# Turning the inverse row sums of a group, and placing its normalised sums, each one slot later in a hand-ordered pipeline

## Chip, cores and metric

The kernel runs on one NeuronCore of a Trainium2 chip. The metric is the device time in microseconds, as the median of several executions; one more execution is recorded by the hardware profiler. All rows below come from that one.

## What is computed

For 8 batches and 8 heads of 576 rows with head width 64, the scores of every row against the 576 keys are formed, all but the 32 largest of a row are dropped, the rest is put through a softmax and multiplied with v. The heads are laid side by side as x (576 rows by 512 per batch), and a channel mix follows, whose input blends each row with the row before it:

```
scores = scale * q @ k.T
kth    = the 32nd largest of each row
attn   = softmax(where(scores >= kth, scores, -1e9))     # row sums + 1e-9 below
x      = (attn @ v), heads side by side
xk, xr = mu*x + (1-mu)*x_prev, for mu_k and mu_r
out    = sigmoid(xr @ w_r) * (relu(xk @ w_k)**2 @ w_v)
```

## The kernel before, in words

**Groups, tiles and slots.** The 4608 rows of all batches are cut in 18 pieces of 256 rows; a piece and a pair of heads make a group, 72 in all. A group has four tiles of 128 partitions (64 rows of each of two heads or row blocks, by 576 scores). There are 288 tiles, and the loop of `pipeline` (line 713) takes one new tile per pass; a pass is called a slot here. Slot n works on tiles of several ages: it forms the scores of tile n, the candidates of tile n-1, the best of tile n-2, the sign count of tile n-3, the exponentials and the threshold mask of tile n-4, and it turns tile n-5 on TensorE (line 284). Each slot emits its steps in the order of the list ORDER (line 43), written out by hand; every engine runs what it was given strictly in that order.

**The row sums.** The mask (L274, VectorE) leaves the masked exponentials and their row sums. Let t be the slot of the last tile of a group. In slot t+5 the four columns of row sums get 1e-9 added (L291, ScalarE), are inverted (L294, VectorE), and each inverse is spread over 64 columns (L298, GpSimd) into the tile rb. In slot t+6 four transposes on TensorE turn rb (L305, `turn_inverse`) into the upper columns of the PSUM tile pt, in which the same slot has just turned another tile; ScalarE moves the result to the tile ri (L309) after it has moved the turned tile (L287). In the same slot, at its end, 40 matmuls weigh v with the turned exponentials of the group (L318). In slot t+7 ScalarE moves those sums out of PSUM (L322), and GpSimd multiplies them by ri (L326, `place`) into xT, the transposed x.

**The channel mix.** It runs beside this, in chunks of 256 rows. A chunk has 8 pieces of gate matmuls (pz), 16 of hidden (ph) and 16 of value (pv), 40 in all; `work` (line 661) lets some into each slot, by a budget of TensorE time per slot (3.45) of which scores, turns, the weighing (1.38) and the turned inverses (0.16) take their part first. Their element-wise steps are queued with a cost on ScalarE ("act") and GpSimd ("pool"), and let in by similar budgets. A half of a chunk may begin once the groups of its two pairs of heads are placed: `state["heads"]` is set in the step place (line 863), and the step mix of the same slot, which comes later in ORDER, looks at it. In the last 36 slots the charge per piece falls from 0.72 to 0.56 (line 673), so that up to four go into a slot. From slot total + 4 on, VectorE takes over from GpSimd for the mix.

**Buffers.** pt has one buffer, so the next slot's turn waits until ScalarE has moved out what lies in it. rb has one buffer, ri and the sums two.

The steps that matter stand in ORDER in this sequence (others left out): count, below, exp, norm, evac, score, turn, inv, keep, sums, bounds, eighth, norm2, et, late, act, thr, mask, place, mix, weigh, dve, pool, judge. "below" is GpSimd's product of scores and signs (L263), "eighth" VectorE's next eight of it (L828), and "late" the move to ri.

Of the kernel before, what the change touches and what calls it, by code (L numbers as in the profile page):

```python
# [46 lines left out]
def topk_attention_channel_mix(ctx: ExitStack, tc: tile.TileContext, q, k, v, mu_k, mu_r, w_k, w_v, w_r, out):  # L47
# [148 lines left out]
    def open_group(P):  # L196
# [4 lines left out]
        for t in range(4):  # L201
            T = Env()
            T.P, T.t, T.u, T.j = P, t, t // 2, t % 2
            T.last = t == 3
            P.tiles.append(T)

    hs = [slice(e * 64, (e + 1) * 64) for e in range(2)]

    def scores(g, P, T):
        x, (Q, R) = T.u * 128, P.blocks[T.u]  # L210
        if Q is R:
            for e, h in enumerate(hs):
                nc.tensor.matmul(g.ps[:, e], lhsT=P.qs[h, T.j, x:x + 128], rhs=Q.K[h, T.j], start=True, stop=True)  # L213
        else:
            for i, N in enumerate((Q, R)):
                for e, h in enumerate(hs):
                    nc.tensor.matmul(g.ps[hs[i], e], lhsT=P.qs[h, T.j, x + i * 64:x + (i + 1) * 64], rhs=N.K[h, T.j], start=True, stop=True)
        return g.ps
# [81 lines left out]
    def turn_inverse(g, P, L):  # L300
        rb = P.rb.rearrange("p (u h) d -> p u (h d)", u=2)
        pr = g.pt[:, :, 384:]
        for u in range(2):
            for n, h in enumerate(hs):
                nc.tensor.transpose(pr[:, n, u * 64:(u + 1) * 64], rb[h, u], ident[h, h])  # L305

        def out_():
            P.ri = g.two.tile([128, 256], F32, name="ri")
            nc.scalar.activation(P.ri.rearrange("p (u n q) -> p n u q", u=2, n=2), pr.rearrange("p n (u q) -> p n u q", u=2), AF.Copy)  # L309
        L.at(0, "late", out_)  # L310
# [13 lines left out]
    def place(P, Q):  # L324
        rows, cols = slice(1 + Q.row, 1 + Q.row + Q.m), slice(Q.c0, Q.c0 + Q.m)
        nc.gpsimd.tensor_mul(Q.xT[:, P.hp, rows], P.sum[:, cols], P.ri[:, cols])  # L326
# [266 lines left out]
    def new_batch(g, b=0):  # L593
        x = g.one.tile([128, HP, 1 + S], F32, name="xT", tag=f"x{b % 2}")
        nc.gpsimd.memset(x[:, :, 0:1], 0.0)
        return x

    def pipeline(g):
        L = Lanes()
# [25 lines left out]
        xT, tiles, state = {}, {}, {"heads": [0] * HP, "wait": 0, "start": 0, "held": [], "K": {}}  # L625

        def save(size=CH):

            b, s = divmod(state["start"], S)
            if s > S - size and not state["held"]:  # L630
                m = S - s
                rest = g.one.tile([128, HP, CH - 63], F32, name="rest")
                nc.gpsimd.tensor_scalar(rest[:, :, :m + 1], xT[b][:, :, s:], 1.0, 1.0, op0=OP.mult, op1=OP.mult)
                state["held"] = [(rest, 0, m)]
# [69 lines left out]
        total = 4 * len(groups)  # L704
# [5 lines left out]
        state["K"][Q.b, P.hp] = Q.K  # L710
        load_mu(L)
        n = 0
        while n < total + 8 or "next" in state or L.busy():
            if n == total + 4:
                g.by, L.rate = nc.vector, 0.5
            A, C, B_, M, V, W = (tiles.get(n - d) for d in (1, 2, 3, 4, 5, 6))
            X = tiles.get(n - EXPS)
            last = W if W and W.last else None
# [38 lines left out]
            def inv():  # L757
                if last:
                    L.use("pe", 1.38)
                if last:  # L760
                    if not V:
                        g.pt = g.psT.tile([128, 2, 512], F32, name="pt")
                    turn_inverse(g, W.P, L)
                    L.use("pe", 0.16)
                    L.use("act", 0.25)

# [77 lines left out]
                    L.use("pool", 0.6)  # L844

            def place_():
                T = tiles.get(n - 7)
                if T and T.last:
                    P = T.P
                    for Q in P.parts:  # L850
                        if Q.b not in xT:
                            if state["start"] < (Q.b - 1) * S:
                                save()
                            C = state["chunk"]
                            assert C.pieces is None or C.begun == 4 or C.first > Q.b - 2
                            assert state["start"] + sum(h[2] for h in state["held"]) >= (Q.b - 1) * S
                            if Q.b > 1:
                                for read in g.reads.values():
                                    L.force(read)
                            xT[Q.b] = new_batch(g, Q.b)  # L860
                        Q.xT = xT[Q.b]
                        place(P, Q)
                    state["heads"][P.hp] = (P.p + 1) * ROWS
                if V and V.last and V.P.last:
                    nc.vector.tensor_reduce(least[:, V.P.p:V.P.p + 1], V.P.group[:, :, :, 23::9], axis=mybir.AxisListType.XYZ, op=OP.min)

            def judge():
                if n == total + 6:
# [4 lines left out]
                    nc.vector.tensor_scalar(flag, lowest, TINY, None, op0=OP.is_lt)  # L873

            do = dict(loads=loads, judge=judge, score=score, turn=turn_, inv=inv, exp=exp, weigh=weigh_, norm=norm, norm2=norm2, bounds=bounds_,
                      count=count_, below=below_, keep=keep_, mix=mix, eighth=eighth, thr=thr, mask=mask_, place=place_, sums=sums, weights=weights)
            do.update({f"c{c}": lambda c=c: cands(c, c + 1) for c in range(NCH)})
            do.update({f"best{r}": lambda r=r: ranks_(best, r) for r in range(3)})
# [10 lines left out]
    with ExitStack() as stack:  # L889
        g = Env()  # L890
        open_pools(stack, g, "")
        stack.enter_context(tc.manual_schedule())
        pipeline(g)
# [3 lines left out]
    with tc.If(again > 0):  # L897
        with tc.For_i(0, B, 1) as b, ExitStack() as stack:
            g = Env()
            g.staged, g.by = (lambda: True), nc.gpsimd  # L900
            open_pools(stack, g, "_again")
            L = Direct()
# [70 lines left out]
```

## Time and profile before

| | us |
|---|---|
| median of 3 runs | 1178.5 (1176.14 to 1180.02) |
| the profiled execution, device time | 1177.31 |
| its span, first to last instruction | 1175.5 |
| TensorE busy with matmuls | 1089.7 (93%) |
| TensorE busy with weight loads | 850.1 (72%) |
| VectorE busy | 1072.5 (91%) |
| ScalarE busy | 966.8 (82%) |
| GpSimd busy | 959.8 (82%) |
| mean granted TensorE clock | 0.982 of full |

The device time holds 1.8 us that lie outside the span. Busy time is a mean over a start (weights are split there, and TensorE has less to do), a long steady part, and an end in which the mix has no attention beside it. The steady part repeats every 16 slots, which is four groups and one chunk.

### The profile page before, as it was taken

The numbers are of one execution on the slowest core, as the hardware profiler recorded it, in microseconds if no ns is written. First come the engines' busy times: TensorE is split into PE (matmuls) and PEld (weight loads), VectorE is DVE, ScalarE is ACT, GpSimd is POOL, SyncE is SP. The second block draws the span as 40 slices with busy tenths as digits, with TensorE's granted clock in tenths as the row PEclk, the third lists the DMA queues.
The fourth block names the chain that finished last, engine by engine and source line by source line (L and its number), as shares of the span: only waits on it lengthen the run. The fifth ranks groups of instructions, "written<-read, shape, count | busy, mean of one in ns | idle before, by whom it ended". The sixth has DMA issues, their size and how long they took to land.

```text
span 1175.5 us, 32787 instructions
## 1 busy us (share of the span) xinstructions
PE 1089.7 (93%) x10753; PEld 850.1 (72%) x10753; DVE 1072.5 (91%) x5959; ACT 966.8 (82%) x1969; POOL 959.8 (82%) x1011
## 2 busy tenths in 40 slices
PE   5678898999999999999999999999999999999897
PEld 2344676868787878787878777878787878777776
DVE  6999999999999999999999999999999998899732
ACT  5898998979897989898989888989898988787721
POOL 4798897888988898989898989898989798787810
PEclk9888999999999999999999999999999999999899
DMA  6433223323332333222221233323232323211000
GB/s 177 133 113 111 54 74 90 81 55 83 84 81 61 79 77 85 59 54 55 71 57 52 57 81 83 78 70 84 76 88 65 86 70 79 78 40 49 11 20 21
DMA packets 168275, 85.86 MB, mean 73 GB/s; under 512 B 126112, under 2 KB 160928, under 8 KB 168096
## 3 DMA queue, kind: packets, MB, share of 16 engines
q1 hardware_dynamic: 168096, 83.67, 27.2%
q8 instruction: 88, 1.44, 0.5%
q14 instruction: 91, 0.75, 0.2%
HBM read 74.19 MB, written 9.44 MB: 71 GB/s over the span
## 4 chain that ended last, share of the span: by engine, by line
PE 43%; POOL 28%; DVE 19%; ACT 5%; issue 3%; DMA 1%; SPq 1%; POOLq 0%; ACTq 0%; DVEq 0%
POOL sg L263 10%; PE ps L318 9%; PE ps L213 6%; DVE cand L246 4%; DVE E L274 4%; PE pv L371 4%; POOL hl L392 3%; PE ph L371 3%; DVE seen L828 3%; POOL xl L367 3%; PE pv L372 3%; PE pv L373 3%; PE pt L284 3%; POOL r L391 3%; PE ph L372 3%
## 5 line engine op out<-in xcount | busy, mean ns | idle before, releaser
L246 DVE MAX8 cand<-sc 128x8 f32<-128x82 f32 (+1 forms) x2016 | 467.2, 232 | 17.9 <-ACT sc L222 17.7
L263 POOL TENSOR_TENSOR sg<-sc,sg 128x576 f32<-128x576 f32 x288 | 410.5, 1428 | 64.2 <-ACT sg L260 61.3
L222 ACT ACTIVATE sc<-ps 128x576 f32<-128x576 f32 x288 | 188.7, 655 | 123.7 <-PE ps L213 108.6
L274 DVE SCALAR_TENSOR_TENSOR E<-sc,seen,se 128x576 f32<-128x576 f32 x288 | 232.9, 809 | 1.4 <-DVE cand L246 0.6
L828 DVE MAX8 seen<-sg 128x8 f32<-128x576 f32 x288 | 216.8, 753 | 18.7 <-POOL sg L263 17.8
L260 ACT ACTIVATE sg<-sc,seen 128x576 f32<-128x576 f32 x288 | 227.5, 790 | 4.1 <-DVE seen L828 3.8
L271 ACT ACTIVATE se<-sc,seen 128x576 f32<-128x576 f32 x288 | 217.8, 756 | 10.1 <-DVE E L274 9.4
L213 PE MATMUL ps<-K,qs 64*128 64x288 f32 x1024 | 200.3, 466 | 18.8 <-ACT sc L222 12.2
L287 ACT ACTIVATE et<-pt 128x640 f32<-128x640 f32 x288 | 205.2, 713 | 14.4 <-PE pt L305 11.0
L284 PEld LDWEIGHTS pt<-ident,E 64*128 64x128 f32 x2880 | 133.5, 139 | 77.1 <-ACT sg L260 16.9
L249 DVE MAX8 seen<-cand 128x8 f32<-128x56 f32 x864 | 177.5, 205 | 0.1
L371 PE MATMUL ph<-xh,wk 128*128 128x256 f32 x576 | 171.5, 298 | 1.2 <-ACT xh L366 1.2
L372 PE MATMUL ph<-xl,wk 128*128 128x256 f32 x576 | 161.2, 280 | 2.5 <-POOL xl L367 2.2
L318 PE MATMUL ps<-et,v_in 128*64 128x128 f32 (+1 forms) x2560 | 160.1, 270 | 3.3 <-ACT sc L222 3.1
L373 PE MATMUL ph<-xh,wk 128*128 128x256 f32 x576 | 160.6, 279 | 0.0
L284 PE MATMUL pt<-ident,E 64*128 64x64 f32 x2880 | 140.3, 224 | 18.9 <-DVE E L274 9.5
L318 PEld LDWEIGHTS ps<-et,v_in 128*64 128x64 f32 x2560 | 133.9, 140 | 27.0 <-issue 13.1
L213 PEld LDWEIGHTS ps<-K,qs 64*128 64x128 f32 x1024 | 79.9, 190 | 86.5 <-issue 27.9
L371 PE MATMUL pv<-wv,hh 128*128 128x512 f32 x288 | 124.8, 433 | 0.0
L252 DVE MATCH_REPLACE8 cand<-seen,cand 128x56 f32<-128x56 f32 x576 | 115.5, 200 | 0.0
L371 PEld LDWEIGHTS ph<-xh,wk 128*128 128x128 f32 x576 | 108.7, 189 | 8.5 <-ACT xh L366 1.6
L372 PE MATMUL pv<-wv,hh 128*128 128x512 f32 x288 | 113.4, 394 | 0.0
(98 smaller groups left out, 2176.7 us busy)
## 6 DMA issues: line engine op xcount, KB each, us to landing
v_in<-in_v SPq DMA_DIRECT2D x192, 128.0 KB, 2.7
K<-in_k SPq DMA_DIRECT2D x112, 144.0 KB, 2.9
qs<-in_q SPq DMA_DIRECT2D x96, 128.0 KB, 2.8
out<-eb SPq DMA_DIRECT2D x36, 256.0 KB, 2.4
vr_in<-in_v SPq DMA_DIRECT2D x96, 32.0 KB, 2.5
hh<-in_moe_w_v SPq DMA_DIRECT2D x6, 512.0 KB, 3.8
qs<-in_q SPq DMA_DIRECT2D x32, 96.0 KB, 2.6
hh<-in_moe_w_k SPq DMA_DIRECT2D x5, 512.0 KB, 4.1
```

Of the source, the lines that this page charges most:

```text
L213: nc.tensor.matmul(g.ps[:, e], lhsT=P.qs[h, T.j, x:x + 128], rhs=Q.K[h, T.j], start=True, stop=True)
L246: nc.vector.max(T.cand[:, 8 * i:8 * i + 8], T.sc[:, CUTS[i]:CUTS[i + 1]])
L260: nc.scalar.activation(T.side, T.sc, AF.Sign, bias=T.top[:, 23:24], scale=-1.0, accum_out=T.cnt)
L263: nc.gpsimd.tensor_mul(T.side, T.sc, T.side)
L271: nc.scalar.activation(g.pe, T.sc, AF.Exp, bias=T.nb, scale=SCALE)
L274: nc.vector.scalar_tensor_tensor(T.e, T.sc, T.thr, g.pe, op0=OP.is_ge, op1=OP.mult, accum_out=T.rs)
L284: nc.tensor.transpose(g.pt[:, n, c * 64:(c + 1) * 64], T.e[h, k0:k0 + 128], ident[h, h])
L287: nc.scalar.activation(et.rearrange("p c (n q) -> p n c q", n=2), pt[:, :, :320].rearrange("p n (c q) -> p n c q", q=64), AF.Copy)
L318: nc.tensor.matmul(g.sums[hs[j], u, q], lhsT=lhsT, rhs=P.et[u, j][:, c, q], start=(c == 0), stop=(c == NKC))
L371: nc.tensor.matmul(ps, lhsT=sh, rhs=mh, start=first, stop=False)
L372: nc.tensor.matmul(ps, lhsT=sh, rhs=ml, start=False, stop=False)
L828: nc.vector.max(M.top[:, 24:32], M.side)
```

## The change

The condition that places the four transposes of rb now looks at the tile seven slots back and no longer six; the charge of 1.38 for the weighing stays in slot t+6. The place step looks at the tile eight slots back. The loop runs on for one slot more. The charges for the sums (`L.use("act", 0.4)` and `L.use("pool", 0.6)`) stay in slot t+7.

```diff
-        while n < total + 8 or "next" in state or L.busy():
+        while n < total + 9 or "next" in state or L.busy():
...
             def inv():
                 if last:
                     L.use("pe", 1.38)
-                if last:
+                X = tiles.get(n - 7)
+                if X and X.last:
                     if not V:
                         g.pt = g.psT.tile([128, 2, 512], F32, name="pt")
-                    turn_inverse(g, W.P, L)
+                    turn_inverse(g, X.P, L)
                     L.use("pe", 0.16)
                     L.use("act", 0.25)
...
             def place_():
-                T = tiles.get(n - 7)
+                T = tiles.get(n - 8)
                 if T and T.last:
```

## Rows read from the trace of the kernel before

**Rows 1.** Windows: length; busy PE, PEld, DVE, ACT, POOL; clock, DMA share, GB/s.

```profile
254.86:965.25 710.39, 691.85 (x7089) 551.67 (x7089) 683.37 (x3925) 619.16 (x1272) 621.77 (x649) 1.00 0.28 73
```

**Rows 2.** Waits from 254.86 to 965.25 us: total us, times, longest us.

```profile
ACT sc L222 <- PE ps L213: 61.9, 69, 3.2
...
POOL xT L326 <- ACT sum L322: 23.0, 16, 2.9
PE pt L305 <- POOL rb L298: 19.9, 22, 1.5
...
DVE seen L828 <- POOL sg L263: 13.0, 30, 0.6
...
DVE rs L294 <- ACT rs L291: 9.1, 12, 0.9
```

**Rows 3.** Waits over the whole span.

```profile
PE pt L305 <- POOL rb L298: 23.2, 25, 1.5
```

**Rows 4.** Chain that ended last, around 611 us: start, us, what.

```profile
609.85 1.38 POOL sg L263
611.23 0.39 POOL rb L298
...
611.66 0.34 PE pt L305 x4
```

**Rows 5.** Timeline of TensorE: start, us, line; scores (L213) open each slot.

```profile
609.26 0.76 PE L213 MATMUL ps<-K,qs 64*128 64x288 f32 x4
...
611.66 0.34 PE L305 MATMUL pt<-ident,rb 64*128 64x64 f32 x4 [1.34 <-POOL rb L298]
...
615.16 0.76 PE L213 MATMUL ps<-K,qs 64*128 64x288 f32 x4
...
618.44 0.76 PE L213 MATMUL ps<-K,qs 64*128 64x288 f32 x4
619.03 0.47 PE L284 MATMUL pt<-ident,E 64*128 64x64 f32 x10
...
639.11 0.76 PE L213 MATMUL ps<-K,qs 64*128 64x288 f32 x4
...
640.00 0.29 PE L305 MATMUL pt<-ident,rb 64*128 64x64 f32 x4
...
643.47 0.76 PE L213 MATMUL ps<-K,qs 64*128 64x288 f32 x4
```

**Rows 6.** Timeline of ScalarE in the same two slots.

```profile
612.64 0.38 ACT L309 ACTIVATE ri<-pt 128x256 f32<-128x256 f32 x1
...
616.02 0.66 ACT L222 ACTIVATE sc<-ps 128x576 f32<-128x576 f32 x1 [1.61 <-PE ps L213]
...
616.83 0.71 ACT L287 ACTIVATE et<-pt 128x640 f32<-128x640 f32 x1
```

**Rows 7.** Timeline of VectorE: two masks, one slot apart.

```profile
612.45 0.80 DVE L274 SCALAR_TENSOR_TENSOR E<-sc,seen,se 128x576 f32<-128x576 f32 x1
...
615.89 0.81 DVE L274 SCALAR_TENSOR_TENSOR E<-sc,seen,se 128x576 f32<-128x576 f32 x1
```

**Rows 8.** GpSimd's groups by shape: busy us, mean ns, idle before.

```profile
L392 POOL TENSOR_TENSOR hl<-r,hh 128x512 fp32r<-128x512 f32 x66 | 85.0, 1287 | 5.2
...
L391 POOL TENSOR_TENSOR r<-r 128x512 f32<-128x512 f32 x66 | 68.8, 1043 | 14.3 <-ACT hh L390 11.8 <-PE ph L373 2.1
```

**Rows 9.** Timeline of the tail, from the last placing on.

```profile
1131.01 0.74 POOL L326 TENSOR_TENSOR xT<-sum,ri 128x256 f32<-128x256 f32 x1 [7.74 <-ACT sum L322]
...
1131.78 0.69 DVE L340 TENSOR_TENSOR xd<-xT 128x512 f32<-128x512 f32 x1 [3.45 <-POOL xT L326]
...
1133.88 1.16 ACT L366 ACTIVATE xh<-xm 128x512 fp32r<-128x512 f32 x2 [2.96 <-DVE xm L350]
...
1138.39 0.69 DVE L412 SCALAR_TENSOR_TENSOR eb<-eb,pv 128x512 f32<-128x512 f32 x1 [3.05 <-PE pv L373]
...
1139.00 1.28 DVE L367 TENSOR_TENSOR xl<-xm,xh 128x512 fp32r<-128x512 f32 x2
```

## The prediction

> **What bounds the kernel now.** I read the windows first, cut at the repeat of 16 slots, since the page's 93% for TensorE and 91% for VectorE mix stages. From 254.86 to 965.25 us lie 12 repeats, of 59.2 us each. There TensorE is busy for 691.85 of 710.39 us and VectorE for 683.37 [rows 1]: 97.4% and 96.2%, 57.7 and 56.9 us a repeat. GpSimd, at 621.77, has 7.4 us of room a repeat. So two engines are nearly full, and each has little to lose.
>
> Next, the waits of the same stretch. TensorE has one wait of size: 19.9 us in 22 cases, all in front of the turned inverses, for GpSimd's spread [rows 2]. That is all its idle time (710.39 - 691.85 = 18.5, within what modelled ends allow). Over the whole span it is 23.2 us in 25 cases [rows 3], so 3.3 lie outside the stretch, all before it. VectorE's 27.0 us of idle time are mainly two waits: 13.0 for GpSimd's product (L263) and 9.1 for ScalarE's 1e-9 step ahead of the reciprocal [rows 2].
>
> Then the chain: at 611 us it runs along GpSimd (product, spread), and crosses from the spread to TensorE at the turned inverses [rows 4]. Once a repeat this is where a backlog of GpSimd is handed on to TensorE. The timeline shows the price: the slot that begins at 609.26 lasts until 615.16, 5.90 us, with the wait of 1.34 in it; the one at 639.11, with the same work of attention but no wait, lasts until 643.47, 4.36 us; an ordinary slot lasts 3.28 (615.16 to 618.44) [rows 5]. ScalarE is passed the delay: its next scores come 1.61 us after it was free [rows 6].
>
> **The change part by part.**
>
> *The turned inverses, one slot later on TensorE.* Four loads and four transposes, 0.29 us in all where nothing is waited for [rows 5], move past this slot's mix pieces, the weighing, and the next slot's scores and turn. Nothing is added. In their new place the spread is a whole slot older: at least 3.28 us, and the longest wait was 1.5 [rows 2, 5]. So all 23.2 us of wait go from this place; that they stay here a slot later, the case that the change doesn't do what it says, I exclude. What is late next: TensorE's own order (no other wait of it is near in the stretch), then the next turn, which needs VectorE's mask. The mask of 612.45 ends at 613.25 [rows 7]; the turn that needs it stood behind the scores of 615.16 and could come 1.9 us earlier. The wait of 1.34 can therefore really be gained on TensorE.
>
> *The move to ri on ScalarE, 0.38 us [rows 6].* It leaves a slot with no other extra move and enters the one with the sums; a shift, no cost in sum. Behind it stand the mix's queued steps and the next slot's sign count. It follows the move of the turned tile, so in the slot of 615.16 it would run at about 617.5 to 617.9 (616.83 + 0.71, + 0.38) [rows 6]. The next turn writes the same single buffer and stands at 619.03 [rows 5]: 1.1 us of cover. Before, the cover was the weighing: from 613.02 to about 615.75, 2.7 us. If the cover goes, TensorE waits at the turn, with the slot's mix pieces behind it. I take zero; the other bound is a rival.
>
> *The placing, one slot later on GpSimd.* Its products, up to 0.74 us each [rows 9], move past the rest of the slot's mix steps and the next slot's product. Before, 23.0 us of waits for the sums stood there [rows 2]; now sums and ri are both old. GpSimd has room at these points, and it waits for ScalarE right behind, so I count nothing for them directly. The memsets and the copy of held rows in the same step move along. No DMA is issued by any moved step, so SP's queue keeps its order.
>
> *The mix, shifted.* Halves of chunks open one slot later, since the heads are set in the step that moves. In the steady part the second half opens in the slot of its placing, and the budget lets in exactly 10 pieces in four slots, 40 in a repeat. Worked along the budget by hand, the first such half (slot 55 and no longer 54) finds GpSimd's budget taken by the hidden steps, its low part comes one slot late, and two pieces find nothing to do. After that the mix has slipped by two pieces, its hidden steps fall on other slots, the second half is let in at once, and nothing more slips. In the last 36 slots I get one slot more to the end. Its price: an ordinary slot holds three pieces in 3.28 - 0.59 (scores to turn) - 0.47 = 2.2 us [rows 5], 0.74 each; at most four pieces, 3.0 us. Those pieces were missing in a slot before, which was shorter for it if TensorE set its pace. Bounds 0 and 3.0; I take the middle, +1.5.
>
> *The shift's second effect.* GpSimd's backlog builds where a slot has a product (1.38), a square (1.04) and a difference (1.29), 3.7 us [rows 4, 8], against VectorE's pace of 3.44 [rows 7]. Before, four such slots fall within five, with a spread in two of them and a placing between; after, within six. Counted slot by slot against VectorE's pace, the largest backlog goes from some 3.9 us to some 3.5. That is in the direction of fewer waits for the product, and small.
>
> *The tail.* The last placing stands at 1131.01; its products end in ScalarE's high part at 1135.04 (1133.88 + 1.16), and the next low part starts only at 1139.00, behind VectorE's output step of 1138.39, which waits for TensorE's last value piece [rows 9]. So a placing up to 4.0 us later is hidden, and a slot in that place is about 3.6. I take zero; without the cover it costs 3.6.
>
> *The sum.* Against the profiled execution's own time of 1177.31 (span 1175.5 and 1.8 around it). If TensorE alone set the pace, the 12 repeats would give back 19.9. VectorE doesn't allow all of it: to follow, it must lose 19.9 of its 27.0 idle, while only the 13.0 and the 9.1 have a cause the change can reach, and both indirectly (an earlier TensorE makes ScalarE's scores, counts and 1e-9 steps earlier, hence GpSimd). The bounds are 0 and 19.9; between them I take a bit under half, 0.8 us of 1.66 a repeat, because the 0.4 us less of backlog and half of the 9.1 / 12 = 0.76 together come to 0.8: -9.6. Of the 3.3 outside, half: -1.6. Slip +1.5. Sum -9.7, so 1167.6; the median stands 1.2 above the profiled execution, so 1168.5 to 1169.
>
> One page of the Trainium skill speaks against this. "Perfetto Trace Analysis", in its section on identifying the most-contended engine, says that matmul busy time is no measure for TensorE, that its weight loads are, and that for VectorE occupancy is; improving means relieving the most contended engine. By it VectorE (96%) is the bound here, TensorE stands at 551.67 of 710.39 (78%), and the sum would be about zero. That is the first rival.
>
> **The rivals.**
>
> *No change: VectorE sets the pace.* Its masks follow each other at 3.44 us for ten slots after 612.45 [rows 7], with no wait of note, while TensorE's 1.34 us are lost. If GpSimd's backlog starts from a step that VectorE times (the spread waits for the reciprocal), an earlier TensorE meets VectorE's waits unchanged: the 19.9 us become waits at the turn for the mask. Against it: VectorE's second wait and ScalarE's 61.9 us for scores [rows 2] hang on TensorE. Time: 1178.5 - 1.6 + 1.5, 1176 to 1179.
>
> *All of it: TensorE sets the pace.* The chain crosses the waits that go [rows 4], which speaks for it; that VectorE would then stand at 99% speaks against. Time: 1178.5 - 23.2 + 1.5 = 1157.
>
> *Slower: the move to ri holds up the next turn.* Place: slot t+8's turn, 1.1 us behind. It decides once ScalarE runs more than 1.1 us later in that slot than at 616.83. The slot now holds both extra moves, and in one group a repeat also a relu step (it stands ahead of the scores). Against it: ScalarE waited 1.61 us for scores in that slot, so it isn't behind [rows 6]. At 0.3 us past the cover in each of 72 groups it costs 21.6, and the time is 1168.8 + 21.6 = 1190.
>
> **How the numbers follow.** Forecast (part of the waits is gained, 1159 to 1174) 0.50; all of it 0.20; no change 0.19; slower through ri 0.08, and through a mix that slips anew in each repeat (two pieces, 1.5 us, 12 times: -9.7 + 18, 1187) 0.03. A measurement here tells 0.3% (3.5 us) from no change. Faster 0.70, same 0.19, slower 0.11. The range takes in the rival that gains all and the one that gains nothing, and leaves out the slower ones: 1156 to 1180.
>
> **What would show it.** Right: no wait of TensorE for the spread; the slot with the weighing at about 4.1 us (4.36 - 0.29) in every group; the repeat at 58.0 to 58.6; VectorE's waits for the product and for the 1e-9 step near 18 us and no longer 22 in 12 repeats; placing without waits; the tail as long as before to within a slot. Wrong: turns that wait for VectorE's mask by about what the spread cost (first rival); turns that wait for L309 (slower); TensorE without any wait at under 57.8 us a repeat (all of it); empty TensorE stretches ahead of gates in each repeat (slip).

## The result, and the profile after

The changed kernel takes 1189.1 us (median of four runs, 1188.0 to 1191.8) against 1177.4 for the kernel before beside it: a ratio of 1.0112, 95% interval 1.0082 to 1.0141. It is slower, where 1168.5 with a gain was forecast, and above the range of 1156 to 1180. Its profiled execution took 1189.53 us, with a span of 1187.6.

Cut at ScalarE's moves of the scores (L222) of slots 96, 240 and 287, the loss lies mostly in the steady part, whose slots 96 to 240 are nine repeats:

| us | before | after |
|---|---|---|
| start to slot 96 | 387.2 | 382.6 |
| slots 96 to 240 | 530.3 | 539.9 |
| slots 240 to 287 | 184.9 | 189.6 |
| slot 287 to the end | 73.2 | 75.5 |

Below, the windows of the changed kernel, from the turned inverses of the same two groups as in [rows 1] (length; busy time of TensorE, its weight loads, VectorE, ScalarE, GpSimd; clock, DMA share, GB/s):

```profile
256.49:975.79 719.30, 697.42 (x7122) 546.91 (x7118) 681.98 (x3917) 629.47 (x1272) 621.25 (x651) 1.00 0.28 72
```

The same work on VectorE (681.98 against 683.37) now takes 719.3 us and no longer 710.4. VectorE's idle time has grown from 27.0 to 37.3. The waits of the changed kernel in that stretch (total us, times, longest) say for whom it waits:

```profile
POOL r L391 <- ACT hh L390: 36.1, 23, 2.9
DVE seen L829 <- POOL sg L263: 35.2, 51, 1.7
...
PE pt L284 <- DVE seen L249: 12.5, 32, 0.6
...
PE ps L318 <- ACT sc L222: 4.5, 10, 0.6
```

TensorE's wait for the spread, 19.9 us in [rows 2], is gone, and so are the placing's 23.0 for the sums and VectorE's 9.1 for the 1e-9 step. In their place VectorE waits 35.2 us for GpSimd's product, where it waited 13.0, and TensorE waits for VectorE at the turn. New at the top is GpSimd itself, which stands 36.1 us at its square of the relu until ScalarE has made its own square. VectorE's 35.2 is the line to look at: its work is as long as before, so what it waits more lengthens the kernel. In the nine repeats it waits 16.5 us more for the product and 6.7 less for the 1e-9 step, 9.8 together, and the nine repeats grew by 9.6.

The change does what it says. The timeline of TensorE in the slots around the second turned inverse (compare [rows 5]):

```profile
639.97 0.76 PE L213 MATMUL ps<-K,qs 64*128 64x288 f32 x4
...
644.18 0.76 PE L213 MATMUL ps<-K,qs 64*128 64x288 f32 x4
...
645.07 0.29 PE L305 MATMUL pt<-ident,rb 64*128 64x64 f32 x4
647.62 0.76 PE L213 MATMUL ps<-K,qs 64*128 64x288 f32 x4
648.20 0.47 PE L284 MATMUL pt<-ident,E 64*128 64x64 f32 x10
```

The slot with the weighing lasts 4.21 us, the next 3.44 with the transposes of rb in it, without a wait. The first was expected at about 4.1.

What went wrong stands in the same 8 us on ScalarE and GpSimd. The second of these slots, from 644.18, is slot 166, the t+7 of its group. The steps to watch are the mix's hidden steps: ScalarE's relu (L388) and its square (L390), then GpSimd's square (L391) and difference (L392). ScalarE's timeline:

```profile
644.20 0.58 ACT L388 ACTIVATE r<-ph 128x512 f32<-128x512 f32 x1
645.04 0.65 ACT L222 ACTIVATE sc<-ps 128x576 f32<-128x576 f32 x1 [0.26 <-PE ps L213]
645.59 0.38 ACT L322 ACTIVATE sum<-ps 128x256 f32<-128x256 f32 x1
645.85 0.72 ACT L287 ACTIVATE et<-pt 128x640 f32<-128x640 f32 x1
646.44 0.41 ACT L309 ACTIVATE ri<-pt 128x256 f32<-128x256 f32 x1
646.70 0.66 ACT L390 ACTIVATE hh<-r 128x512 fp32r<-128x512 f32 x1
```

The relu of the mix's hidden part stands ahead of the scores, its square behind the scores, the sums, the turned tile and ri: 2.5 us from the one's start to the other's. GpSimd's timeline:

```profile
641.99 2.79 POOL L263 TENSOR_TENSOR sg<-sc,sg 128x576 f32<-128x576 f32 x2
647.43 1.04 POOL L391 TENSOR_TENSOR r<-r 128x512 f32<-128x512 f32 x1 [2.65 <-ACT hh L390]
648.55 1.29 POOL L392 TENSOR_TENSOR hl<-r,hh 128x512 fp32r<-128x512 f32 x1
649.80 1.44 POOL L263 TENSOR_TENSOR sg<-sc,sg 128x576 f32<-128x576 f32 x1
651.20 0.72 POOL L326 TENSOR_TENSOR xT<-sum,ri 128x256 f32<-128x256 f32 x1
652.00 1.04 POOL L340 TENSOR_TENSOR xd<-xT 128x512 f32<-128x512 f32 x1
...
655.21 1.42 POOL L263 TENSOR_TENSOR sg<-sc,sg 128x576 f32<-128x576 f32 x1
```

It makes two products in a row with nothing between, then stands 2.65 us at the square, and is full from there on, with the placing and the first steps of a chunk (L340 and on) in one slot. Before, the second pair of hidden steps stood between those two products, in slot 165, and nothing waited in slot 166:

```profile
642.39 1.04 POOL L391 TENSOR_TENSOR r<-r 128x512 f32<-128x512 f32 x1
643.51 1.29 POOL L392 TENSOR_TENSOR hl<-r,hh 128x512 fp32r<-128x512 f32 x1
644.74 1.45 POOL L263 TENSOR_TENSOR sg<-sc,sg 128x576 f32<-128x576 f32 x1
646.13 0.76 POOL L326 TENSOR_TENSOR xT<-sum,ri 128x256 f32<-128x256 f32 x1
```

In the changed kernel the product of 655.21, in slot 168, is late for VectorE:

```profile
651.84 0.75 DVE L829 MAX8 seen<-sg 128x8 f32<-128x576 f32 x1
...
656.66 0.76 DVE L829 MAX8 seen<-sg 128x8 f32<-128x576 f32 x1 [1.28 <-POOL sg L263]
```

In the nine repeats GpSimd waits 27.1 us at its square, where it was 2.0 before; 24.3 of them are nine waits in this very slot. Of VectorE's 25.8 us for the product, 9.3 stand in slots like 168, where none stood before. Another 8.9 (3.7 before) stand four slots on, in slots like 172:

```profile
673.48 0.76 DVE L829 MAX8 seen<-sg 128x8 f32<-128x576 f32 x1 [1.38 <-POOL sg L263]
```

There the fourth pair of hidden steps has moved from slot 168 to 169, and the next two slots are full of the mix's other steps and the placing. So there are two places where the product has become late, and only the first lies behind GpSimd's standing.

So the theory to test, called S in the expectations: the mix has slipped by two pieces, because its second halves open a slot later; that takes the second pair of hidden steps from the slot of the weighing (t+6) to slot t+7, where GpSimd, which takes its work in order, stands still behind ScalarE. The rivals: the turned inverse and its move in a slot with the sums (R), the placing in its new place (P), and, later, the late and heaped begin of a chunk (L).

### The profile page after: what moved, and what is told of

Read it like the earlier page. It is cut to its first block, busy times and chain, and to the rows that moved or that the text cites. A ratio compares the mean times of both kernels' runs of the same rounds, so it can differ in the third digit from the quotient of the medians.

```text
span 1187.6 us, 32795 instructions
## 1 busy us (share of the span) xinstructions
PE 1103.3 (93%) x10753; PEld 850.8 (72%) x10753; DVE 1074.7 (90%) x5961; ACT 979.2 (82%) x1969; POOL 956.1 (81%) x1009
## 3 DMA queue, kind: packets, MB, share of 16 engines
q1 hardware_dynamic: 168096, 83.67, 26.6%
## 4 chain that ended last, share of the span: by engine, by line
PE 40%; POOL 27%; DVE 20%; ACT 8%; issue 2%; SPq 1%; DMA 1%; POOLq 0%; ACTq 0%; DVEq 0%
POOL sg L263 9%; PE ps L318 8%; PE ps L213 6%; DVE E L274 5%; PE ph L371 4%; DVE cand L246 4%; DVE seen L829 4%; PE ph L372 4%; POOL hl L392 3%; PE pt L284 3%; PE ph L373 3%; POOL xm L350 3%; POOL r L391 3%; POOL xm L345 3%; POOL xl L367 3%; PE pv L371 3%
## 5 line engine op out<-in xcount | busy, mean ns | idle before, releaser
L829 DVE MAX8 seen<-sg 128x8 f32<-128x576 f32 x288 | 216.7, 752 | 41.7 <-POOL sg L263 41.2
L222 ACT ACTIVATE sc<-ps 128x576 f32<-128x576 f32 x288 | 187.8, 652 | 76.5 <-PE ps L213 70.6
L213 PE MATMUL ps<-K,qs 64*128 64x288 f32 x1024 | 201.2, 468 | 15.4 <-ACT sc L222 10.4
L284 PE MATMUL pt<-ident,E 64*128 64x64 f32 x2880 | 144.5, 228 | 33.9 <-DVE seen L249 21.4
L318 PEld LDWEIGHTS ps<-et,v_in 128*64 128x64 f32 x2560 | 134.5, 140 | 32.6 <-ACT sc L222 25.1
L213 PEld LDWEIGHTS ps<-K,qs 64*128 64x128 f32 x1024 | 80.1, 190 | 83.3 <-issue 35.3
```

The lines of the kernel that those rows point to most:

```text
L284: nc.tensor.transpose(g.pt[:, n, c * 64:(c + 1) * 64], T.e[h, k0:k0 + 128], ident[h, h])
L318: nc.tensor.matmul(g.sums[hs[j], u, q], lhsT=lhsT, rhs=P.et[u, j][:, c, q], start=(c == 0), stop=(c == NKC))
L829: nc.vector.max(M.top[:, 24:32], M.side)
```

## The experiments

All ratios are to the kernel before, run beside each kernel; "nine repeats" are slots 96 to 240 as above.

| kernel | us | ratio, interval | nine repeats | TensorE for spread | GpSimd at square / placing | VectorE for product |
|---|---|---|---|---|---|---|
| before | 1177 to 1179 | | 530.3 | 14.2 | 2.0 / 15.1 | 9.3 |
| after | 1189.1 | 1.0112 (1.0082 to 1.0141) | 539.9 | none | 27.1 / none | 25.8 |
| e1 signal late | 1200.0 | 1.0201 (1.0160 to 1.0241) | 549.4 | 18.7 | 5.0 / 45.0 | 20.8 |
| e2 inverse late | 1164.9 | 0.9891 (0.9863 to 0.9920) | 521.8 | none | 2.6 / 12.2 | 9.0 |
| e3 placing late | 1203.2 | 1.0212 (1.0184 to 1.0239) | 551.6 | 25.8 | 29.8 / none | 26.6 |
| e4 plan kept | 1215.2 | 1.0329 (1.0298 to 1.0359) | 556.6 | none | 9.1 / none | 25.1 |
| e5 ri behind | 1186.2 | 1.0096 (1.0064 to 1.0127) | 537.4 | none | 24.2 / none | 22.9 |
| e6 square apart | 1175.6 | 0.9971 (0.9951 to 0.9991) | 530.9 | none | 3.0 / none | 16.7 |
| e7 behind weighing | 1166.0 | 0.9920 (0.9890 to 0.9949) | 523.4 | none | 4.6 / 5.1 | 8.6 |
| e8 inverse, signal late | 1183.9 | 1.0069 (1.0045 to 1.0093) | 535.3 | none | none / 41.7 | 20.5 |
| e9 two pieces | 1187.9 | 1.0082 (1.0055 to 1.0109) | 535.2 | none | none / 41.4 | 20.2 |
| e10 inverse, square apart | 1165.2 | 0.9885 (0.9856 to 0.9914) | 521.5 | none | none / 14.5 | 8.8 |
| e11 four slots | 1169.8 | 0.9931 (0.9904 to 0.9958) | 523.3 | none | 0.9 / none | 0.2 |
| e12 held four | 1172.2 | 0.9953 (0.9934 to 0.9972) | 523.2 | none | 6.2 / 29.8 | 1.6 |

**e1, the signal alone.** Only the mix's knowledge of a placed group is a slot late:

```diff
-                    state["heads"][P.hp] = (P.p + 1) * ROWS
...
+                T = tiles.get(n - 8)
+                if T and T.last:
+                    state["heads"][T.P.hp] = (T.P.p + 1) * ROWS
```

> The kernel before, with one thing late: the mix learns of a placed group one slot later. Inverses are turned and sums placed in the slots of before. Theory S (the mix slips by two pieces, so that the hidden steps fall on other slots and GpSimd's square waits for ScalarE's; the product behind it is late for VectorE): at least as slow as the changed kernel, 1186 to 1198, with TensorE's waits for the spread still there, GpSimd's waits at its square (L391) over 20 us in nine repeats and VectorE's waits for the product over 20. Rival R (the turned inverse and its move to ri, in a slot that also moves the sums, make ScalarE late): as before, 1175 to 1180. Rival P (the placing in its new slot on GpSimd): as before, 1175 to 1180.

1200.0: the late signal by itself costs twice what the whole change costs, and R and P, which expected nothing, fall as main causes. But one link of S was wrong. The waits of e1 in nine repeats:

```profile
POOL xT L326 <- ACT sum L322: 45.0, 24, 4.4
DVE seen L828 <- POOL sg L263: 20.8, 40, 1.1
PE pt L305 <- POOL rb L298: 18.7, 13, 2.1
...
POOL r L391 <- ACT hh L390: 5.0, 15, 0.5
```

GpSimd waits at the placing and not at the square: where the placing still stands ahead of the square in slot t+7, it waits there for the sums (14.2 of the 45.0 us in slots like 166, the rest in the t+7 of other groups). The step that it stands at is whichever comes first; what stays is that GpSimd stands.

**e2, the inverse alone.** The change of `inv`, with the placing left at `n - 7`.

> Half of the change: inverses are turned one slot later, sums are placed in the slot of before, after the move to ri of the same slot, so that the mix keeps its plan. Theory S: no slower than before, 1165 to 1177, with no wait of TensorE for the spread and VectorE's wait for the product at or under 13 us in nine repeats, though GpSimd now waits about 1 us longer at each placing. Rival R: slower, 1184 to 1192. Rival P: 1165 to 1178, as Theory S.

1164.9, the fastest kernel here together with e10, and at the lower end of S. This half of the change gains 12.8 us. VectorE's wait for the 1e-9 step is gone, its wait for the product is as before, and TensorE's 14.2 us for the spread are gone; the largest wait that it has now is 5.7 us for ScalarE's move of the scores. The placing, which S expected to wait some 1 us longer each time, waits less than before (12.2 for 15.1 us):

```profile
POOL xT L326 <- ACT ri L309: 12.2, 17, 1.6
DVE seen L829 <- POOL sg L263: 9.0, 20, 0.7
...
PE ps L318 <- ACT sc L222: 5.7, 16, 0.5
```

**e4, the plan kept by letting the begin of a chunk in without charge.**

```diff
-            l = [L.soft("pool", 0.0046 * n + 0.05 * len(pieces), change, *l, rank=1)]
+            l = [L.soft("pool", 0.0, change, *l, rank=1)]
```

(share and add alike, where `which` is 1).

> The whole change, but the first steps of a chunk on GpSimd (difference, share, sum for the gates) are let in without charge, so that the hidden steps of the mix keep the slots they had before; the price is a heap of those steps in the slot of the placing. Theory S: the loss goes, 1165 to 1180, with GpSimd's waits at its square under 8 us in nine repeats. Rival R: still slow, 1184 to 1192. Rival P: still slow, 1184 to 1194.

1215.2, a miss for every theory. The hidden steps kept their slots, but the difference, two shares and the sum came in the slot of the placing beside a square and its difference, and VectorE's waits for the product, 25.1 us, are fewer and longer (18, up to 2.9):

```profile
POOL sg L263 <- ACT sg L260: 60.8, 45, 3.4
PE ps L318 <- ACT sc L222: 27.0, 10, 3.4
DVE seen L829 <- POOL sg L263: 25.1, 18, 2.9
```

The kernel exchanged one fault for a larger one, so it tells nothing on R and P; it shows what it can cost to let steps past the budget on GpSimd.

**e6, the whole change with GpSimd's square in its own tile.**

```diff
-        q = L.soft("pool", 1.17, lambda: g.by.tensor_mul(X.r[:, :, :n], X.r[:, :, :n], X.r[:, :, :n]), h, rank=-1)
+        def square():
+            X.rr = g.one.tile([128, 2, CH], F32, name="rr")
+            g.by.tensor_mul(X.rr[:, :, :n], X.r[:, :, :n], X.r[:, :, :n])
+        q = L.soft("pool", 1.17, square, h, rank=-1)
...
```

(The difference behind it then reads `X.rr`.)

> The whole change, with GpSimd's square written to a tile of its own, so that it no longer waits until ScalarE's square has read the relu; the plan of the slots is that of the changed kernel. Theory S, with GpSimd's wait at the square as the link: GpSimd's waits there fall from 27 us in nine repeats to under 8 (the difference behind it then waits a little), VectorE's wait for the product falls by 5 to 15, and the time to 1176 to 1186. If that wait only stands in for GpSimd's load in the new slots: 1187 to 1191. Rivals R and P: 1187 to 1191.

1175.6, 13.5 under the changed kernel, with the same plan. The square no longer has to wait until ScalarE has read r; the difference behind it waits instead, but shorter:

```profile
DVE seen L832 <- POOL sg L263: 16.7, 29, 1.6
POOL hl L395 <- ACT hh L390: 13.6, 9, 1.7
...
POOL rr L393 <- ACT r L388: 3.0, 9, 0.5
```

27.1 us of waiting became 16.6, VectorE's 25.8 became 16.7, and nine repeats became 9.1 shorter. So GpSimd's standing in slot t+7 is a cause and not a companion. It isn't the whole: the nine repeats are still 9.1 us longer than e2's. VectorE's waits in slots like 168 fell from 9.3 to 2.1 us, those in slots like 172 stayed (8.9 and 8.8).

**e9, the slip alone, on top of e2.** In one slot of the whole kernel two pieces are held back:

```diff
-                work(MOST)
+                work(MOST if n != 59 else 1)
```

> The second kernel of this series (inverse late, placing as before: 1164.9) with one thing more: in one slot, number 59, two pieces of matmuls of the mix are held back, once. The signal of a placed group stays on time. Theory S (the slip of two pieces, which takes the second pair of hidden steps from the slot of the weighing to slot t+7, is the whole loss): 1178 to 1195, with GpSimd's waits for ScalarE in slot t+7 and VectorE's waits for the product over 18 us in nine repeats; two pieces alone are worth 1.5. Rival L (what costs is the late begin of a chunk's second half and its heap of GpSimd steps, not where the hidden steps lie): 1163 to 1170.

1187.9: 23.0 us above e2, for two pieces of 0.74 us held back once. The signal is on time here, so the slip alone is enough. It doesn't tell S from L, though: the hidden steps stand in the slots of the changed kernel, but so do the first steps of a chunk on GpSimd, all four of the second half's together in slot 167, where e2 has three in slot 166 and the last in 169. The waits in nine repeats:

```profile
POOL xT L326 <- ACT ri L309: 41.4, 24, 2.3
...
DVE seen L829 <- POOL sg L263: 20.2, 39, 1.1
```

GpSimd stands 16.9 of the 41.4 us in slots like 166, and 20.3 in slots like 162, the t+7 of the group before. A repeat is 1.5 us longer in the mean (535.2 against 521.8 for nine): the slip isn't caught up, because the budget fills exactly 40 pieces into 16 slots, and so every later chunk has its hidden steps in the wrong slots. Of the rest, 3.2 us lie in slots 240 to 287 and 4.8 behind slot 287; these were not taken apart.

**e11, the whole change with the mix four slots later.** Eight more pieces held back once, so that the hidden steps stand again where they stood within a group:

```diff
-                work(MOST)
+                work({60: 0, 61: 0, 62: 0, 63: 2}.get(n, MOST))
```

> The whole change, with eight more pieces held back once, in slots 60 to 63, so that the mix is four slots later than before and its hidden steps stand on the same slots of a group as before; inverse and placing stay one slot late. Theory S: the loss goes, and the wait for the spread too: 1160 to 1172, as the kernel with the inverse alone. Rival L: 1160 to 1172 as well, since halves now open long before they are needed. Rival P (placing in slot t+8 is itself late for something): 1180 to 1195. Rival R (the move to ri in a slot with the sums): 1180 to 1195.

1169.8: holding back more work makes the changed kernel 19 us faster. VectorE's waits in nine repeats:

```profile
DVE rs L294 <- ACT rs L291: 5.5, 9, 0.8
...
DVE seen L829 <- POOL sg L263: 0.2, 1, 0.2
```

The wait for the product is gone. Inverse and placing are where the change put them, so P and R are no more than small. The heap of a chunk's first steps behind the placing still stands in slot 167, as in the changed kernel, but no hidden step stands ahead of it in slots 165 and 166:

```profile
636.75 0.74 POOL L326 TENSOR_TENSOR xT<-sum,ri 128x256 f32<-128x256 f32 x1
637.57 1.04 POOL L340 TENSOR_TENSOR xd<-xT 128x512 f32<-128x512 f32 x1
638.72 0.94 POOL L345 TENSOR_SCALAR xm<-xd,nmu 128x256 f32<-128x256 f32 x2
639.74 1.09 POOL L350 TENSOR_TENSOR xm<-xm,xT 128x512 f32<-128x512 f32 x1
```

So the heap alone makes no loss. With e6, where heap and late begin stay and 13.5 us go, L is at most a part.

**e3, the placing alone.** Only `place_` at `n - 8` (and the loop's end).

> The other half of the change: sums are placed one slot later, inverses are turned in the slot of before. The plan of the mix slips as in the changed kernel. Theory S: as the first kernel of this series, or a little under it, 1186 to 1204, with TensorE's waits for the spread near 18 us in nine repeats; placing no longer waits for the sums (45 us there). If halves simply add up (1189.1 + 12.8 for the inverse): 1202. If the wait of the placing made most of the 1200: 1180 to 1190.

1203.2, and the halves add up to within 1 us: 12.8 gained by e2 and 25.2 lost here give 1189.8, and 1189.1 was measured.

**e10, e2 with e6's tile.**

> Inverse late, placing as before, and GpSimd's square in a tile of its own. In the kernel with the inverse alone that square waited only 2.6 us in nine repeats, so if what the square in its own tile gave the changed kernel (1189 to 1175.6) was that kernel's wait and nothing else, there is nothing to gain: 1162 to 1167. If a tile of its own helps in itself: under 1160.

1165.2, as e2: where the square doesn't wait, a tile of its own gains nothing.

**e5, the move to ri behind the mix's steps.** In `turn_inverse`, `L.at(0, "early", out_)` for `L.at(0, "late", out_)`.

> The whole change, with the move to ri behind the mix's steps of its slot on ScalarE, and no longer ahead of them: ScalarE's square comes 0.3 to 0.4 us sooner in slot t+7. Rival R in its small form (the move to ri is what makes GpSimd's square wait): 27 us of waits in nine repeats fall to under 10 and the time to under 1181. Theory S (the slot is the cause: scores, sums and the turned tile stand ahead of the square with or without ri): 24 us fall by 9 times 0.4, about 3.6, and the time by 0 to 4: 1185 to 1190.

1186.2, with 24.2 us of waits at the square for 27.1: the 0.3 us a slot that S expected. In the waits R is a tenth of the matter; the time can't be told from the changed kernel's, as the intervals overlap.

**e8, all but the placing itself.** e2 with e1's late signal.

> The whole change but for the placing itself: inverse late, signal to the mix late, sums placed in slot t+7 as before. Theory S: like the changed kernel, 1185 to 1195, since the slip is the same; a placing that stands in slot t+7 and waits there for ri can only add. Rival P (the placing's new place on GpSimd has a cost of its own): well under it, 1165 to 1182.

1183.9, a little under what S expected and above what P did. Its nine repeats are those of e9 (535.3 and 535.2), so in the steady part the late signal acts through the slip alone. Against the changed kernel (1.0069 and 1.0112, intervals that overlap) the placing's own share, up to 5 us, stays open.

**e7, another way to the same gain.** Before's plan, with the turned inverses behind the weighing of the same slot, and the move to ri ahead of the next scores (`L.at(1, "evac", out_)`).

```diff
                     for u in range(2):
                         weigh(g, W.P, u)
+                    if not V:
+                        g.pt = g.psT.tile([128, 2, 512], F32, name="pt")
+                    turn_inverse(g, W.P, L)
...
```

> The kernel before with the turned inverses behind the weighing of slot t+6 (some 3 us later on TensorE and no longer in a slot of their own), and the move to ri ahead of the scores of slot t+7, where ScalarE waits anyway. Placing, and with it the plan of the mix, are those of before. Theory S: the wait for the spread goes, the placing waits for the sums alone: 1160 to 1168, at least as fast as the inverse alone (1164.9). Against it: the next turn on TensorE now has only the scores (0.6 us) as cover for the move to ri; if that is short by 0.3 us in each of 72 groups, 1175 to 1190.

1166.0: the gain of e2 within the intervals, without a slot's delay. The short cover at the next turn showed, but on ScalarE (17.8 us of waiting for the transposes, in 31 cases) and not in the time.

**e12, e2 held back by four slots.** `work({59: 1, 60: 0, 61: 0, 62: 0, 63: 2}.get(n, MOST))`.

> Inverse late and placing as before, and the mix held back by ten pieces once, in slots 59 to 63, so that it runs four slots later with its hidden steps on the same slots of a group. Theory S: the hidden steps' slots in a group are those of the kernel with the inverse alone (1164.9), so the steady part is at least as fast; the second halves now open well ahead, and VectorE's wait for the product, 9.0 us in nine repeats there, falls to under 3 as in the whole change held back by four slots (0.2). The end of the kernel takes up to 3 us more. 1157 to 1166.

1172.2, a miss. The wait for the product went to 1.6 us as expected, but nine waits for the 1e-9 step came back (5.2), the placing waits 29.8, and the end from slot 240 on takes 6 us longer than e2's. Beside e11, which has the same plan of the mix with the placing a slot later (0.9931 and 0.9953, intervals that overlap), the later placing costs nothing that shows. Best of all kernels tried are e2 and e10, 1.1% faster than before.

## Why the prediction was wrong

**The step that failed is "the mix, shifted".** The slip itself was worked out rightly: two pieces once, before the second chunk's hidden steps, never caught up, no second slip. Its price was put as the time of the pieces, +1.5 with 3.0 as the upper bound. Measured by e9 against e2 it is +23.0, which with the -12.8 of e2 makes +10.2 of the +11.7 of the whole change. A slip doesn't cost its pieces; it costs what every later chunk's steps wait for in the slots where they come to stand. The next part, "the shift's second effect", did look at those slots, but counted GpSimd's load against VectorE's pace alone, and found 0.4 us less backlog. It left out that a step of GpSimd in slot t+7 must wait for a ScalarE that has scores, sums, a turned tile and ri ahead, and that the product queued behind stands with it. Freeing the square of that wait gives 13.5 us back (e6). It also left out that the fourth pair of hidden steps would crowd slots 169 to 172, which e6 leaves as it is; how much of the remaining time that costs was not tried by itself. A row pointed to the first of these: in [rows 2] the placing waited 23.0 us. Most of it stands in the t+7 of the last group of a repeat (12.5 of 15.1 us in nine repeats), where GpSimd comes early; in slots like 166 GpSimd came late, and nothing waited. I read those 23.0 as a wait that goes, and not as a sign of what a step meets that comes early in a slot t+7.

**The inverse, one slot later: right, and the size near.** -11.2 was forecast for the waits (-9.6 and -1.6); e2 measured -12.8. The detail was off: of VectorE's two waits the one for the 1e-9 step went wholly and the one for the product not at all, where half of the one and 0.4 us a repeat of backlog were counted on. A repeat takes 58.0 us in e2, as forecast (58.0 to 58.6), and 60.0 in the changed kernel.

**The move to ri: right.** No turn waits for it in the changed kernel, and its share of the loss is small (e5). **The placing: right that its wait goes.** Its own place costs up to 5 us beside the slip (the changed kernel against e8) and nothing that shows in e11; the signal that goes with it is what the slip comes from.

**The tail: nearly right.** The last placing and its followers after the change:

```profile
1141.15 0.74 POOL L326 TENSOR_TENSOR xT<-sum,ri 128x256 f32<-128x256 f32 x1 [8.15 <-ACT ri L309]
...
1143.99 0.67 DVE L340 TENSOR_TENSOR xd<-xT 128x512 f32<-128x512 f32 x1
...
1150.45 0.69 DVE L412 SCALAR_TENSOR_TENSOR eb<-eb,pv 128x512 f32<-128x512 f32 x1 [3.82 <-PE pv L373]
1151.06 1.29 DVE L367 TENSOR_TENSOR xl<-xm,xh 128x512 fp32r<-128x512 f32 x2
```

The low part still starts behind VectorE's output step, so the later placing is hidden, as in [rows 9]. The part from slot 287 on is 2.3 us longer, within the slot that was forecast.

**The rivals.** The slower one with a slipping mix ("slips anew in each repeat", 0.03) named the right part and a wrong mechanism: nothing slips anew (the hidden steps stand in the same slots of every repeat from slot 68 to 248), and TensorE stands empty ahead of the gates for only 4.7 us, in four of the 12 repeats. That its time of 1187 is near the measured one is luck. The other slower one fell. "VectorE sets the pace" expected the waits for the spread to come back as waits at the turn. In part they do in the changed kernel (12.5 us), but in the nine repeats of e2 no such wait is left, and the time falls. The reading under that rival was wrong too: of the nine gaps between VectorE's masks after 612.45, on [rows 7], several are longer than 3.44 us; they go from 3.41 to 4.04, with a mean of 3.63. The count of GpSimd's backlog went by the same 3.44.

The Trainium skill's "Perfetto Trace Analysis", in its section on optimization strategy, advises to find the gaps on the engine that is being optimized and what blocks it there. Here the trace agrees: VectorE's wait for the product went from 9.0 to 20.2 us where e9 lost 23.0, and from 25.8 to 0.2 where e11 gained 19.3. The rule that the prediction drew from that page of the Trainium skill, to relieve the most contended engine, does not by itself give a sum of zero, as the prediction read it. In e2 TensorE's wait was taken away, and with it went VectorE's wait of 6.7 us for the 1e-9 step: VectorE's idle time in nine repeats fell from 17.9 to 10.7 us, most of the 8.5 that they became shorter.

## What to carry to other kernels

In a pipeline whose order is written out ahead, a step that moves carries its signals with it: ask which budgeted work those let in, in which slot each of its steps then stands, and what the first step of an in-order queue will wait for there. Price a slip by that, and not by its pieces. And where two edits come together, measure each alone: here one was worth 12.8 us and the other lost twice that.

## What was not expected of the hardware

The first two tell more of this kernel's schedule than of the chip. Two pieces of matmuls held back once cost 23.0 us (e9 against e2), and eight more held back gave 19 of the changed kernel's time back (e11). Removing a single order on one tile (ScalarE reads the relu before GpSimd overwrites it) gave 13.5 us (e6), with no instruction fewer on any engine. The granted TensorE clock of the part from slot 287 on was 0.96 of full before and 0.93 after, so the changed kernel spent more of it at the lower of the two levels (1.2 GHz); in slots 240 to 287 it was 0.98 and 0.95. Whether that made part of the 2.3 and 4.7 us by which these parts are longer was not tried; the nine repeats ran at 1.00 in both.
